# Four accumulator tiles, more idle products, and exponentials read tile by tile from the bank: one change to an attention and gated MLP kernel

## The chip, the cores and the metric

One core of a Trainium2 chip runs the whole program. The metric is the device time of one execution in microseconds (us). TensorE (PE) multiplies, VectorE (DVE), ScalarE (ACT) and GpSimd (POOL) do the elementwise work, and SyncE (SP) issues most transfers. Each engine works through its own list of instructions in order and waits at semaphores for the others.

## The reference

```python
# q, k, v: [8, 8, 576, 64] float32; the head's number sets its mask
scores = q @ k.T / 8
mask_plain = (rel >= 0) & (rel < 32)                                # heads 0 to 3, rel = i - j
mask_dil = (rel >= 0) & (rel < 128) & (rel % 4 == 0)                # heads 4 to 7
scores = where(mask, scores, -1e9); scores -= max(scores)
attn = exp(scores); attn /= sum(attn) + 1e-9
x = (attn @ v) laid out as [4608 tokens, 512]
h = x @ w_in                                                        # w_in [512, 2048]
g = h * sigmoid(1.702 h)
out = g @ w_out                                                     # w_out [2048, 512]
```

The inputs of the MLP arrive as 8-byte floats. They are decoded on the chip into a high and a low part, and every MLP product is the sum of three (high by high, low by high, high by low).

## The kernel before

**Tiling.** Heads are worked on in pairs, four pairs to a batch entry, 32 in all. A pair `k` has scores of 128 rows by 2 heads by 5 tiles (`QT`) of 64 columns. Pairs 0 to 3 (`first_attention`) give the input of the first group of the MLP, so they stand at the head of the program; pairs 4 to 7 (`attention`) are spread over that group, and the other 24 over the later groups. The MLP works in nine groups of 512 tokens: `m0` to `m7` and `r` (the tokens left over). A group runs 16 steps `f`: `up(f)` is 12 products of 512 columns into the bank `hp`, then ACT does a tanh (L605), DVE a gating product (L608), ACT or DVE the high part `gh` and DVE the low part `gl`; `down(f)` adds 12 products into four accumulators of 512 columns each, `acc`. In the last step of a group each accumulator `j` is finished by three products (L633, L634, L637) and drained by ACT into `ost_m` or `ost_r` (L226, from `add_out`), and then stored.

**The accumulators.** All four are one tile, `accs`, of four banks. The first four pairs use the same tile for `first_product` (L462).

**Softmax of pairs 0 to 7** (`masked(k)`): the mask is added by two products with `ident` ahead of the scores, so the bank `sp` holds masked scores. Then DVE takes the maximum (L394), DVE subtracts it (L233, `pr<-sp,mx`, 640 elements), ACT takes the exponential of all 640 (L398), and DVE sums (L412). The bank `sp` is free for the next pair's scores after the subtraction. A reciprocal, a product on POOL or DVE, and DVE transposes into `ct` follow.

**Decoding a weight tile** (`decode`) takes a 512 KB transfer, two ACT shifts (L281, L282), a sign step on DVE or ACT (L277 or L275), and further steps on DVE, ACT and POOL. There are 32 such tiles, all decoded in the head and the first group.

**What sets the order.** `Plan` gathers every operation with a cost for each engine that can do it, and an urgency. `ordered` builds a list for each engine from these costs, once, ahead of the run. So a change of a cost number or an urgency moves instructions between and along the engines. In the head it also puts in `idle` products (L719) on PE where it expects PE to wait: into the bank `hp`, until `up(0)` of the first group has taken that bank.

The names of buffers in the profile are `cell`, `second`, `bt` (undecoded weights), `words` (a decode's middle step), `wih`, `wil`, `woh`, `wol` (decoded weights), `xh`, `xl` (the MLP's input, high and low).

Of the kernel before, what the change touches and what calls it, by code (L numbers as in the profile page):

```python
# [22 lines left out]
AHEAD = 0.6  # L23
WARM = 30.0
# [10 lines left out]
LATER = {PE: 0.0, ACT: 0.0, DVE: 0.4, POOL: 0.0, DMA: 0.0}  # L35
# [3 lines left out]
class Plan:  # L39
# [29 lines left out]
    def ordered(self, warm, warm_until, soon):  # L69
# [24 lines left out]
        while any(open_):  # L94
# [43 lines left out]
def tile_windowed_attention_then_gated_mlp(  # L138
# [49 lines left out]
    accs = bank([P, NC, GT], "acc", "acc")  # L188
# [52 lines left out]
    def decode(n, urgency):  # L241
# [38 lines left out]
        add({DMA: 524}, {0: -7.0, 1: -5.0, 2: -3.5, 3: -2.5}.get(n, urgency), fetch, (), (R, R + "l", *taken))  # L280
# [41 lines left out]
    def load_v(k):  # L322
        u, place = pairs[k], lots(k)[1]

        def work(e):
# [13 lines left out]
            (place, place + "l"), (0.0, 6.0, 8.0, 10.0)[k] if k < NC else 0.0)  # L339
# [38 lines left out]
    def exponentials(k, urgency):  # L378
# [3 lines left out]
        held = ("sp",) if masked(k) else ()  # L382

        def sp():
            return u["all"] if masked(k) else pr

        if not masked(k):
            mine = mask if dilated(k) else plain
            for n, tiles, cost in ((P, slice(0, QT - 1), 0.62), (D, slice(QT - 1, QT), 0.22)):
                add({DVE: cost}, urgency, lambda e, n=n, tiles=tiles: pair(  # L390
                    e, pr[0:n, :, tiles], u["all"][0:n, :, tiles],
                    mine[0:n, None, tiles].broadcast_to([n, 2, tiles.stop - tiles.start, W]), ALU.add),
                    ("sp",), (PR,))
        add({DVE: 0.80}, urgency, lambda e: V.tensor_reduce(out=mx, in_=sp(), axis=AX.X, op=ALU.max),  # L394
            held or (PR,), (MX,))
        add({DVE: 0.80}, urgency, lambda e: pair(
            e, pr, sp(), mx[:, :, :, None].broadcast_to([P, 2, QT, W]), ALU.subtract), (*held, MX), (PR,))
# [8 lines left out]
    def softmax(k, urgency):  # L406
# [5 lines left out]
        add({DVE: 0.80}, urgency, lambda e: V.tensor_reduce(out=sm, in_=pr, axis=AX.X, op=ALU.add), (PR,), (SM,))  # L412
        inverse(k, urgency)
        for a in range(2):
            add({POOL: 0.73, DVE: -0.48}, urgency, lambda e, a=a: pair(
# [30 lines left out]
    def first_product(k):  # L446
# [6 lines left out]
        u["x"] = accs[:, :, ROW * (k % 2):ROW * (k % 2) + ROW]  # L453
# [24 lines left out]
    def drain_x(k, urgency):  # L478
# [19 lines left out]
        if b == 0:  # L498
# [8 lines left out]
            for n, (size, part, src) in enumerate(mains):  # L507
                add({ACT: 0.12 + size * 0.00094}, urgency, lambda e, part=part, src=src: copy(
# [56 lines left out]
    class Group:  # L565
# [119 lines left out]
    for c in range(NC):  # L685
        first_attention(c, c)
        if c in (1, 2):
            decode(c - 1, c + 2.5)
# [79 lines left out]
```

## Time and profile before

| | |
|---|---|
| median of 3 runs | 924.18 us (923.68 to 924.65) |
| the profiled execution | 923.53 us, of which the profile's span is 921.8 us |
| PE busy | 888.0 us (96%) |
| DVE, ACT, POOL busy | 450.3, 386.0, 71.7 us |
| instructions | 17123, of them 7313 products |

PE is busy nearly throughout, so the two places to look at are the stretches in which it is not, and those in which its clock is low. The head of the program (the first 40 us) and the ends of the nine groups are where PE's idle time lies. ACT and DVE are close to full from 40 to 115 us, where the weights are decoded, and half idle later.

### The profile page before, as it was taken

How to read it: one execution, taken by the hardware profiler on the slowest of the kernel's cores; microseconds unless marked ns; L12 is line 12 of the kernel's file. 1: busy time of each engine (PE TensorE's matmuls, PEld its weight loads, DVE VectorE, ACT ScalarE, POOL GpSimd, SP SyncE). 2: the span in 40 equal slices, each digit the busy share in tenths (PEclk: the TensorE clock that was granted, in tenths of full speed). 3: DMA queues.
4: the chain of work that ended last, by engine and by line, in shares of the span. 5: the costliest groups of instructions: out<-in, count | busy, mean ns of one | idle time of the engine just before them, and what ended most of it. 6: DMA issues, size and time to landing. Idle time of an engine off the chain costs nothing.

```text
span 921.8 us, 17123 instructions
## 1 busy us (share of the span) xinstructions
PE 888.0 (96%) x7313; PEld 714.7 (78%) x7313; DVE 450.3 (49%) x844; ACT 386.0 (42%) x669; POOL 71.7 (8%) x86
## 2 busy tenths in 40 slices
PE   6899999999999999999999999999999999999997
PEld 4577777888788878888788878887888778878885
DVE  6799985564556254634564255525422412232221
ACT  5889874343543244323443244424422322232222
POOL 3312220010001000000010000100000000000000
PEclk9799999999999999999999999999999999999999
DMA  9366742211221012300311023101000010001001
GB/s 347 126 223 179 246 134 91 92 46 46 91 92 46 1 64 73 92 0 16 122 46 47 1 91 91 46 1 44 24 1 1 2 44 1 1 14 32 1 1 46
DMA packets 35803, 61.32 MB, mean 67 GB/s; under 512 B 17424, under 2 KB 17680, under 8 KB 35728
## 3 DMA queue, kind: packets, MB, share of 16 engines
q1 hardware_dynamic: 35584, 60.11, 20.3%
q8 instruction: 57, 0.93, 0.4%
q14 instruction: 18, 0.15, 0.1%
q10 hardware_dynamic: 144, 0.13, 0.0%
HBM read 49.48 MB, written 9.44 MB: 64 GB/s over the span
## 4 chain that ended last, share of the span: by engine, by line
PE 90%; ACT 5%; DMA 2%; DVE 1%; issue 1%; SPq 0%; ACTq 0%
PE hp_m L597 37%; PE acc L637 14%; PE acc L633 14%; PE acc L634 13%; PE hp_r L597 5%; PE av L476 3%; PE sp L375 3%; ACT ost_m L226 2%; DMA cell<-wo_dram 1%; PE acc L462 1%; DMA cell<-wi_dram 1%; DMA second<-wo_dram 1%; ACT words L281 1%; ACT second L275 1%; ACT gh L226 0%
## 5 line engine op out<-in xcount | busy, mean ns | idle before, releaser
L633 PE MATMUL acc<-gh,woh 128*128 128x512 f32 x576 | 226.9, 394 | 4.9 <-ACT ost_m L226 4.1
L634 PE MATMUL acc<-gh,wol 128*128 128x512 f32 x576 | 224.4, 390 | 0.0
L597 PE MATMUL hp_m<-xh,wih 128*128 128x512 f32 x512 | 203.8, 398 | 2.8 <-ACT xh L226 1.9
L597 PE MATMUL hp_m<-xl,wih 128*128 128x512 f32 x512 | 201.4, 393 | 0.3 <-DVE xl L233 0.2
L597 PE MATMUL hp_m<-xh,wil 128*128 128x512 f32 x512 | 201.3, 393 | 0.0
L608 DVE SCALAR_TENSOR_TENSOR g_m<-g_m,hp_m 128x512 f32<-128x512 f32 x128 | 87.8, 686 | 230.3 <-ACT g_m L605 229.9
L637 PE MATMUL acc<-gl,woh 128*128 128x512 f32 x576 | 162.3, 394 | 13.7 <-ACT ost_m L226 11.7
L605 ACT ACTIVATE g_m<-hp_m 128x512 f32<-128x512 f32 x128 | 76.6, 599 | 234.4 <-PE hp_m L597 233.9
L637 PEld LDWEIGHTS acc<-gl,woh 128*128 128x128 f32 x576 | 107.6, 188 | 44.3 <-ACT ost_m L226 19.0
L633 PEld LDWEIGHTS acc<-gh,woh 128*128 128x128 f32 x576 | 108.1, 188 | 31.1 <-ACT ost_m L226 6.1
L634 PEld LDWEIGHTS acc<-gh,wol 128*128 128x128 f32 x576 | 108.2, 188 | 21.9
L233 DVE TENSOR_TENSOR gl<-g_m,gh 128x512 fp32r<-128x512 f32 x126 | 89.1, 707 | 58.1 <-ACT gh L226 52.9
L597 PEld LDWEIGHTS hp_m<-xh,wih 128*128 128x128 f32 x512 | 97.0, 190 | 25.5 <-DVE g_m L608 3.1
L597 PEld LDWEIGHTS hp_m<-xl,wih 128*128 128x128 f32 x512 | 97.2, 190 | 22.1 <-DVE xl L233 1.4
L597 PEld LDWEIGHTS hp_m<-xh,wil 128*128 128x128 f32 x512 | 97.1, 190 | 20.1 <-POOL wil L233 0.6
L226 ACT ACTIVATE gh<-g_m 128x512 fp32r<-128x512 f32 x117 | 73.9, 632 | 68.8 <-DVE g_m L608 68.6
L233 POOL TENSOR_TENSOR pr<-pr,sm 128x320 f32<-128x320 f32 x64 | 52.4, 840 | 520.8 <-DVE sm L404 516.6
L226 ACT ACTIVATE bt<-ct 32x320 f32<-32x320 f32 x101 | 47.5, 470 | 14.3 <-DVE ct L425 12.4
L226 ACT ACTIVATE xm<-av 128x512 f32<-128x512 f32 (+2 forms) x42 | 24.5, 594 | 44.8 <-PE av L476 31.5
L608 DVE SCALAR_TENSOR_TENSOR g_r<-g_r,hp_r 128x512 f32<-128x512 f32 x16 | 11.0, 688 | 53.6 <-ACT g_r L605 53.6
L398 ACT ACTIVATE pr<-pr 128x640 f32<-128x640 f32 x32 | 23.7, 740 | 30.9 <-DVE pr L233 30.8
L412 DVE TENSOR_REDUCE sm<-pr 128x10 f32<-128x640 f32 x32 | 26.2, 817 | 13.3 <-ACT pr L398 13.3
(114 smaller groups left out, 717.6 us busy)
## 6 DMA issues: line engine op xcount, KB each, us to landing
qk<-qk_dram SPq DMA_DIRECT2D x17, 576.0 KB, 4.8
out_dram<-ost_m SPq DMA_DIRECT2D x31, 256.0 KB, 2.0
second<-qk_dram SPq DMA_DIRECT2D x13, 576.0 KB, 4.3
v<-vp_dram SPq DMA_DIRECT2D x32, 216.0 KB, 4.3
words<-vp_dram SPq DMA_DIRECT2D x24, 216.0 KB, 4.4
cell<-wi_dram SPq DMA_DIRECT2D x10, 512.0 KB, 5.6
cell<-wo_dram SPq DMA_DIRECT2D x9, 512.0 KB, 4.4
second<-wo_dram SPq DMA_DIRECT2D x6, 512.0 KB, 5.2
```

What stands on the lines that cost most here:

```text
L226: A.activation(dst, src, AF.Copy, scale=scale)
L233: (V if e == DVE else G).tensor_tensor(out=dst, in0=a, in1=b, op=op)
L375: T.matmul(dst[:, w:w + n], u["qk"][rows, at:at + 32], u["qk"][rows, S + first:S + first + n], start=not masked(k), stop=True, tile_positi ...
L398: add({ACT: 0.75}, urgency, lambda e: A.activation(prs[y], prs[y], AF.Exp, scale=0.125), (), (PR,))
L412: add({DVE: 0.80}, urgency, lambda e: V.tensor_reduce(out=sm, in_=pr, axis=AX.X, op=ALU.add), (PR,), (SM,))
L476: T.matmul(dst, u["v"][a][0:KW, m], bt[0:KW, a, m], start=True, stop=True, skip_group_check=True)
L597: T.matmul(hps[f], st[:, f, c], mv[:, c], start=c == 0 and k == 0, stop=c == NC - 1 and k == 2)
L605: A.activation(self.g32, hps[f], AF.Tanh, scale=0.851)
L608: V.scalar_tensor_tensor(out=self.g32, in0=self.g32, scalar=1.0, in1=hps[f], op0=ALU.add, op1=ALU.mult)
L633: T.matmul(self.acc[j], woh[:, f, cols], gh, start=f == 0, stop=False)
L634: T.matmul(self.acc[j], wol[:, f, cols], gh, start=False, stop=False)
L637: T.matmul(self.acc[j], woh[:, f, P * j:P * j + P], self.g[f][1], start=False, stop=f == NF - 1)
```

## The change

1. **Accumulators.** `accs` goes. A tile `first_x` of four banks serves the first four pairs; then its pool is closed, and each accumulator `j` of each group is a tile of its own, in a bank of its own (`quarter`).
2. **Exponentials of pairs 0 to 7.** The subtraction, the one exponential of 640 and the sum go. DVE scales the ten maxima of a row by -0.125 (10 elements), and ACT takes the exponential of each of the 10 tiles straight from the bank `sp`, 64 elements at a time, with the scaled maximum as bias and with the sum as a second output. The bank is free after the last tile.
3. **Idle products.** They go to the bank `av` and may be put in until pair 4's `product` has taken it; the allowance ahead of a wait grows (0.5 us taken off instead of 1.5), and the last planned time from 30 to 36 us.
4. **Numbers of the plan.** Urgencies of the decodes and of pairs 4 to 7, slacks of the first `v`, costs of scores, first products, drains and POOL's product are other numbers. The plan's cost for five tiles of exponentials is 0.80. The up products of the first group wait for both parts of `xh` and `xl`.

```diff
-AHEAD = 0.6
-WARM = 30.0
+AHEAD = 0.70
+WARM = 36.0
...
-                idle = max(0, int((when - max(free[e], 1.2) - 1.5) / (0.28 if when > 5.0 else 0.44)))
+                idle = max(0, int((when - max(free[e], 1.2) - 0.5) / (0.26 if when > 8.0 else 0.44)))
...
-    accs = bank([P, NC, GT], "acc", "acc")
+    four = tc.tile_pool(name="four", bufs=1, space=bass.MemoryType.PSUM)
+    first_x = four.__enter__().tile([P, NC, GT], F32, tag="x", name="first_x")
+
+    def quarter(j, name):
+        if "quarters" not in misc:
+            four.__exit__(None, None, None)
+            misc["quarters"] = ctx.enter_context(tc.tile_pool(name="quarters", bufs=1, space=bass.MemoryType.PSUM))
+        return misc["quarters"].tile([P, GT], F32, tag=f"acc{j}", name=name)
...
-        add({DVE: 0.80}, urgency, lambda e: V.tensor_reduce(out=mx, in_=sp(), axis=AX.X, op=ALU.max),
-            held or (PR,), (MX,))
+        if masked(k):
+
+            sm, SM = sms[y], f"sm{y}"
+            add({DVE: 0.80}, urgency, lambda e: V.tensor_reduce(out=mx, in_=u["all"], axis=AX.X, op=ALU.max),
+                ("sp",), (MX,))
+            add({DVE: -0.15}, urgency, lambda e: V.tensor_scalar(
+                out=mx, in0=mx, scalar1=-0.125, scalar2=None, op0=ALU.mult), (), (MX,))
+            for a in range(2):
+                def tiles_of(e, a=a):
+                    for t in range(QT):
+                        A.activation(pr[:, a, t], u["all"][:, a, t], AF.Exp, bias=mx[:, a, t:t + 1], scale=0.125,
+                                     accum_out=sm[:, a, t:t + 1])
+
+                add({ACT: 0.80}, urgency, tiles_of, ("sp", MX), (PR, SM))
+            return
...
-        add({DVE: 0.80}, urgency, lambda e: V.tensor_reduce(out=sm, in_=pr, axis=AX.X, op=ALU.add), (PR,), (SM,))
+        if not masked(k):
+            add({DVE: 0.80}, urgency, lambda e: V.tensor_reduce(out=sm, in_=pr, axis=AX.X, op=ALU.add), (PR,), (SM,))
...
-                    self.acc[j] = accs[:, j]
+                    self.acc[j] = quarter(j, f"acc_{self.name}_{j}")
...
-                decode(n, 25.0 + 2.3 * n)
+                decode(n, 28.0 + 2.62 * n)
...
-                    attention(NC + c, 50.0 + 10.0 * c)
+                    attention(NC + c, 43.0 + 8.2 * c)
...
-        if 0 not in main[0].hps:
+        if "av" not in pairs[NC]:
             if "idle" not in misc:
-                misc["idle"] = bank([P, GT], "hp", "idle")
+                misc["idle"] = bank([P, GT], "av", "idle")
```

**Where it moves instructions.** First, PE's list at the end of the first group, the last `down` before `up(1)` of the next group, with the semaphores that each row waits for. Before:

```order
L637 MATMUL acc<-gl_75,woh 128x512 [waits Pool_49]
L633 MATMUL acc<-gh_73,woh 128x512
L634 MATMUL acc<-gh_73,wol 128x512
L637 MATMUL acc<-gl_75,woh 128x512 [waits Activation_49]
L633 MATMUL acc<-gh_73,woh 128x512
L634 MATMUL acc<-gh_73,wol 128x512
L637 MATMUL acc<-gl_75,woh 128x512 [waits Activation_49]
L633 MATMUL acc<-gh_73,woh 128x512
```

The same place of the change:

```order
L654 MATMUL acc_m_0_749<-gl_75,woh 128x512 [waits DVE_49]
L650 MATMUL acc_m_1_754<-gh_73,woh 128x512
L651 MATMUL acc_m_1_754<-gh_73,wol 128x512
L654 MATMUL acc_m_1_754<-gl_75,woh 128x512
L650 MATMUL acc_m_2_758<-gh_73,woh 128x512
L651 MATMUL acc_m_2_758<-gh_73,wol 128x512
L654 MATMUL acc_m_2_758<-gl_75,woh 128x512
L650 MATMUL acc_m_3_764<-gh_73,woh 128x512
```

The products stand in the same order; the two waits for ACT among them are gone.

Second, ACT's list in the head, from the first decode step on (buffer numbers 78, 79 are the `pr` of even and odd pairs). Before:

```order
L281 ACTIVATE words<-cell_109 128x512
L282 ACTIVATE cell_109<-cell_109 128x512
L398 ACTIVATE pr_78<-pr_78 128x640
L281 ACTIVATE words<-cell_110 128x512
L398 ACTIVATE pr_79<-pr_79 128x640
L226 ACTIVATE wih<-words 128x512
L282 ACTIVATE cell_110<-cell_110 128x512
L281 ACTIVATE words<-cell_111 128x512
```

The change:

```order
L289 ACTIVATE words<-cell_112 128x512
L290 ACTIVATE cell_112<-cell_112 128x512
L283 ACTIVATE cell_112<-cell_112 128x512
L400 ACTIVATE pr_78,sm_82<-sp_142,mx_80 128x64 x5
L289 ACTIVATE words<-cell_113 128x512
L400 ACTIVATE pr_78,sm_82<-sp_142,mx_80 128x64 x5
L290 ACTIVATE cell_113<-cell_113 128x512
L289 ACTIVATE words<-cell_114 128x512
L290 ACTIVATE cell_114<-cell_114 128x512
L400 ACTIVATE pr_79,sm_83<-sp_230,mx_81 128x64 x5
```

Ten small exponentials stand where one stood, with decode steps among them, and the sign step of the first tile (L283) has come from DVE to ACT. Up to the tanh of the first group's first step, ACT's list has 35 instructions before (from its first decode step on), four of them exponentials; the change has 40 tiles of exponentials and 33 others. On PE, ahead of the first `down`, stand 27 products of `up` before and 33 in the change; and 9 idle products before against 39, of which 15 lie between the scores of pairs 0 and 1, and 10 after the scores of pair 1. On SP the first weight tile's transfer goes from third to second place.

More of the change, by code (lines that the diff above doesn't have):

```diff
@@ L34 @@
 PE, ACT, DVE, POOL, DMA = range(5)
-LATER = {PE: 0.0, ACT: 0.0, DVE: 0.4, POOL: 0.0, DMA: 0.0}
+LATER = {PE: 0.0, ACT: 0.0, DVE: 0.40, POOL: 0.0, DMA: 0.0}
 LATENCY = {PE: 0.3, ACT: 0.2, DVE: 0.2, POOL: 0.2, DMA: 0.2}
@@ L338, in load_v @@
         add({DMA: 390 if k < NC else 442}, (-5.5, -3.0, -2.0, -1.0)[k] if k < NC else 1.6 * k - 0.3, work, waits(k),
-            (place, place + "l"), (0.0, 6.0, 8.0, 10.0)[k] if k < NC else 0.0)
+            (place, place + "l"), (0.0, 1.0, 5.0, 14.0)[k] if k < NC else 0.0)
     def waits(k):
@@ L381, in exponentials @@
         PR, MX = f"pr{y}", f"mx{y}"
[L382 to L394, printed above, removed]
-            held or (PR,), (MX,))
+        if masked(k):
[11 more added lines that the diff above has]
+            return
+        mine = mask if dilated(k) else plain
+        for n, tiles, cost in ((P, slice(0, QT - 1), 0.62), (D, slice(QT - 1, QT), 0.22)):
+            add({DVE: cost}, urgency, lambda e, n=n, tiles=tiles: pair(
+                e, pr[0:n, :, tiles], u["all"][0:n, :, tiles],
+                mine[0:n, None, tiles].broadcast_to([n, 2, tiles.stop - tiles.start, W]), ALU.add),
+                ("sp",), (PR,))
+        add({DVE: 0.80}, urgency, lambda e: V.tensor_reduce(out=mx, in_=pr, axis=AX.X, op=ALU.max), (PR,), (MX,))
         add({DVE: 0.80}, urgency, lambda e: pair(
-            e, pr, sp(), mx[:, :, :, None].broadcast_to([P, 2, QT, W]), ALU.subtract), (*held, MX), (PR,))
+            e, pr, pr, mx[:, :, :, None].broadcast_to([P, 2, QT, W]), ALU.subtract), (MX,), (PR,))
         add({ACT: 0.75}, urgency, lambda e: A.activation(prs[y], prs[y], AF.Exp, scale=0.125), (), (PR,))
@@ L411, in softmax @@
         exponentials(k, urgency)
-        add({DVE: 0.80}, urgency, lambda e: V.tensor_reduce(out=sm, in_=pr, axis=AX.X, op=ALU.add), (PR,), (SM,))
+        if not masked(k):
+            add({DVE: 0.80}, urgency, lambda e: V.tensor_reduce(out=sm, in_=pr, axis=AX.X, op=ALU.add), (PR,), (SM,))
         inverse(k, urgency)
         for a in range(2):
-            add({POOL: 0.73, DVE: -0.48}, urgency, lambda e, a=a: pair(
+            add({POOL: 0.85, DVE: -0.48}, urgency, lambda e, a=a: pair(
                 e, pr[:, a], pr[:, a], sm[:, a, :, None].broadcast_to([P, QT, W]), ALU.mult), (SM,), (f"{PR}.{a}",))
@@ L507, in drain_x @@
             for n, (size, part, src) in enumerate(mains):
-                add({ACT: 0.12 + size * 0.00094}, urgency, lambda e, part=part, src=src: copy(
+                add({ACT: 0.12 + size * (0.0019 if dilated(k) else 0.00094)}, urgency, lambda e, part=part, src=src: copy(
                     e, part(xh[:, c]), src()), FOUR, (f"xh{c}.{n}",))
-                add({DVE: 0.08 + size / 640}, urgency, lambda e, part=part, src=src: pair(
+                add({DVE: 0.08 + size / (490 if dilated(k) else 820)}, urgency, lambda e, part=part, src=src: pair(
                     e, part(xl[:, c]), src(), part(f32(xh[:, c])), ALU.subtract), (*FOUR, f"xh{c}.{n}"), (f"xl{c}.{n}",))
@@ L599, in up @@
             for c in range(NC):
-                split = [f"x{k}{c}.{n}" for k in "hl" for n in range(1)] if self is main[0] else []
+                split = [f"x{k}{c}.{n}" for k in "hl" for n in range(2)] if self is main[0] else []
                 add({PE: 0.681}, 0.0, lambda e, c=c: product(c), (f"wi{f}", f"xh{c}", f"xl{c}", *split), (place,))
@@ L687, in tile_windowed_attention_then_gated_mlp @@
         if c in (1, 2):
-            decode(c - 1, c + 2.5)
+            decode(c - 1, c + 0.1)
     last, nxt = None, 1
```

10 lines of the change are left out of this document (5 added, 5 removed).

## The prediction

> **What bounds the kernel now.** I read the page's first lines, then the waits of TensorE (PE), then the timeline around the longest group of waits, then busy time by stretches.
>
> ```profile
> span 921.8 us, 17123 instructions
> PE 888.0 (96%) x7313; PEld 714.7 (78%) x7313; DVE 450.3 (49%) x844; ACT 386.0 (42%) x669; POOL 71.7 (8%) x86
> ```
>
> PE is the bound over the whole run, so a gain has to come from its 34 us of idle time or from stretches in which it runs slowly. The view of waits names the idle time (total, times, longest):
>
> ```profile
> PE acc L637 <- ACT ost_m L226: 11.7, 17, 0.7
> PE acc L633 <- ACT ost_m L226: 4.1, 6, 0.7
> PE acc L637 <- ACT ost_r L226: 2.1, 3, 0.7
> PE acc L462 <- issue: 2.0, 1, 2.0
> PE hp_m L597 <- ACT xh L226: 1.9, 2, 1.2
> PE hp_m L597 <- DVE g_m L608: 0.7, 1, 0.7
> PE acc L633 <- ACT gh L226: 0.6, 2, 0.3
> ```
>
> The first three lines are 26 waits of 0.69 us: products into the accumulators that wait for ACT to drain one. They all lie at ends of groups. The timeline of the last one (start, length, instruction, idle time before it) shows what one costs:
>
> ```profile
> 138.86 0.60 ACT L226 ACTIVATE ost_m<-acc 128x512 f32<-128x512 f32 x1 [0.47 <-PE acc L634]
> ...
> 915.37 0.50 PE L637 MATMUL acc<-gl,woh 128*128 128x512 f32 x1 [0.69 <-ACT ost_m L226]
> 915.71 0.39 PE L633 MATMUL acc<-gh,woh 128*128 128x512 f32 x1
> 915.94 0.40 PE L634 MATMUL acc<-gh,wol 128*128 128x512 f32 x1
> 917.03 0.50 PE L637 MATMUL acc<-gl,woh 128*128 128x512 f32 x1 [0.69 <-ACT ost_m L226]
> ```
>
> A product follows the one before it after 0.23 us (915.71 to 915.94). Where the wait is, the step is 1.09 us (915.94 to 917.03), and the step after a wait is 0.34 us (915.37 to 915.71). So one wait costs 0.86 + 0.11 = 0.97 us, more than the 0.69 us that is called idle, since the pipeline runs empty. The product that waits goes into another accumulator than the one being drained: the drain starts when the next accumulator's first products end (the 0.47 us wait for L634 at 138.86), and the third product of that accumulator waits for the drain. That is an order among accesses to one tile, not one that the data need.
>
> Busy time by stretches, cut at ACT's first decode step, at the first, eighth and sixteenth tanh of the first group (columns: length, PE, PEld, DVE, ACT, POOL busy and instructions, clock, DMA share, GB/s):
>
> ```profile
> 8.13:38.93 30.80, 24.81 (x641) 16.84 (x642) 23.43 (x49) 22.34 (x35) 12.05 (x12) 0.83 0.63 238
> 38.93:77.11 38.18, 37.27 (x305) 29.21 (x304) 35.47 (x67) 35.47 (x55) 6.64 (x6) 1.00 0.57 181
> 77.11:132.75 55.64, 54.87 (x571) 42.78 (x570) 50.15 (x97) 46.59 (x77) 9.96 (x10) 1.00 0.73 219
> 132.75:921.80 789.05, 766.92 (x5706) 624.04 (x5704) 337.98 (x623) 279.08 (x500) 41.76 (x51) 1.00 0.13 41
> ```
>
> In the head PE is idle for a fifth of the time and waits for the softmax of pairs 0 to 3. In the second row PE is nearly full, but ACT and DVE are at 93% too: what is added there to one of them turns soon into time. In the third row ACT has 9 us to spare, in the last one more than half.
>
> **The accumulators.** With a tile for each, the 26 waits go: 26 x 0.97 = 25.2 us. What is late next? A drain takes 0.60 us and the three products of an accumulator 3 x 0.23 = 0.69 us, so ACT keeps pace behind PE. The next group's first product into the same bank now waits for that drain, but 12 products of `up(1)` (2.7 us) stand between. The next group's `gh` needs tanh, gating product and copy behind up to four drains on ACT, some 4 us after `up(0)`; PE has 24 products (5.5 us) in between. I take no new wait.
>
> **The exponentials: DVE.** For each of eight pairs the subtraction and the sum go, and a product of ten elements comes:
>
> ```profile
> 7.40 0.82 DVE L233 TENSOR_TENSOR pr<-sp,mx 128x640 f32<-128x640 f32 x1
> ...
> 10.04 0.82 DVE L412 TENSOR_REDUCE sm<-pr 128x10 f32<-128x640 f32 x1
> 10.77 0.81 DVE L394 TENSOR_REDUCE mx<-sp 128x10 f32<-128x640 f32 x1
> 11.50 0.16 DVE L402 TENSOR_SCALAR sm<-sm 128x10 f32<-128x10 f32 x1
> ```
>
> From start to start a large one takes 0.73 us, so DVE is relieved of 2 x 0.73 - 0.16 = 1.3 us a pair. This shortens nothing by itself, since ACT gets the work.
>
> **The exponentials: ACT.** The one exponential of 640 goes and ten of 64 come. Nothing in the trace shows an exponential with a bias read from memory or with a sum. The nearest rows are a copy of 64 elements out of a bank, and the exponential:
>
> ```profile
> 20.99 0.23 ACT L226 ACTIVATE xr<-acc 128x64 f32<-128x64 f32 x1
> 21.09 0.64 ACT L226 ACTIVATE woh<-words 128x512 fp32r<-128x512 f32 x1
> 21.62 0.70 ACT L281 ACTIVATE words<-bt 128x512 f32<-128x512 f32 x1
> ...
> 12.70 0.73 ACT L398 ACTIVATE pr<-pr 128x640 f32<-128x640 f32 x1
> 13.32 0.62 ACT L226 ACTIVATE wih<-words 128x512 fp32r<-128x512 f32 x1
> ...
> 15.42 1.33 ACT L275 ACTIVATE cell<-cell 128x512 f16<-128x512 f32 x1
> 16.50 0.72 ACT L282 ACTIVATE cell<-cell 128x512 uint32<-128x512 uint32 x1
> ```
>
> The copy holds ACT for 0.10 us until the next starts, and lasts 0.23 us by itself. So a tile, T, costs at least 0.10 us; and if each runs alone, and giving out its sum takes a further instruction of that size, 0.46 us. I take the middle, 0.28 us, since both additions cost something and nothing says that they prevent all overlap. A pair is then 2.8 us on ACT in place of 0.62 us.
>
> The Trainium skill, "ScalarE: Activation LUTs", section "What ACT_TABLE_LOAD costs", says that a bias read through a pointer adds about 93 ns to an ACTIVATE and that neighbours overlap by about 93 ns; by its figures a tile would be an estimated 0.24 us, and the time predicted below 2.4 us less (60 tiles x 0.04); it has no price for the sum that is given out.
>
> *In the head.* ACT's list from its first decode step to the first tanh was 35 instructions, 22.3 us, of which the four exponentials were 4 x 0.62. The change has 33 others: two more of some 0.55 us and a little, so about 21.4 us, and 40 tiles. It can start earlier, since the first weight tile is fetched second:
>
> ```profile
> 8.13 0.67 ACT L281 ACTIVATE words<-cell 128x512 f32<-128x512 f32 x1 [2.91 <-DMA cell<-wi_dram]
> ...
> 38.93 0.60 ACT L605 ACTIVATE g_m<-hp_m 128x512 f32<-128x512 f32 x1 [0.88 <-PE hp_m L597]
> ...
> 41.73 0.50 PE L633 MATMUL acc<-gh,woh 128*128 128x512 f32 x1
> ...
> 5.00:10.00 5.00, 4.15 (x172) 2.70 (x177) 2.67 (x4) 2.09 (x4) 0.00 (x0) 1.00 1.02 408
> ```
>
> The 0.59 MB that now come after it are 1.4 us at 408 GB/s, so ACT starts at 6.7. With 1.2 us of waiting (it had single waits above 2 us before; I take about half of one) the first tanh comes at 6.7 + 21.4 + 40 x 0.28 + 1.2 = 40.5 us, against 38.93: 1.6 us later. Following the softmax of the four pairs by hand gives the same: each pair holds the bank longer, but after the fourth ACT still has some 8 us of decode steps and copies ahead of the tanh. The first `down` follows 2.8 us after the tanh, as now. By then PE has done 33 instead of 27 products of `up`: 6 x 0.23 = 1.4 us that needn't be done later. Head: +0.2 us.
>
> *Up to the eighth tanh.* ACT's list loses a sign step (1.08 us, 15.42 to 16.50), two exponentials and a copy (0.53, 21.09 to 21.62; together about 2.8 us) and gains 20 tiles (5.6 us). ACT goes from 35.5 to 38.3 us. PE would need 38.2 - 1.4 = 36.8 us there. So ACT, full, takes the head's gain back: +1.5 us. Up to the sixteenth, the list loses seven instructions besides the exponentials, and the 20 tiles fill that; the 9 us of room cover it. If that room were gone, it would be up to 3 us.
>
> **The idle products.** They were 0.43 us apart (an inference from two taking 1.03 us and three 1.46 us), so the 15 between the scores of pairs 0 and 1 fill 6.5 us, from 6.5 to 13.0:
>
> ```profile
> 6.44 1.03 PE L719 MATMUL idle<-ident 128*128 128x512 bf16 x2
> ...
> 27.00:28.00 1.00, 0.99 (x3) 0.56 (x3) 1.00 (x3) 1.00 (x2) 0.00 (x0) 0.51 0.81 319
> 36.00:37.00 1.00, 1.00 (x4) 0.71 (x4) 1.00 (x2) 1.00 (x3) 0.00 (x0) 0.50 0.00 0
> 37.00:38.00 1.00, 1.00 (x5) 0.87 (x4) 1.00 (x3) 1.00 (x2) 0.00 (x0) 0.88 0.00 0
> ```
>
> The second scores wait for the first ten tiles of exponentials, until about 12.6, so the products are hidden; with tiles of 0.10 us they would hold the scores up by 2 us. What they may buy is the clock, which was granted at half from 27 to 37 us. I count that as nothing: after the change ACT's list, not PE, decides when the tanh comes.
>
> The Trainium skill, "TensorE: Matmul & The Clock Gate", Part 1, has the clock fall to half after an idle window of about 3.4 us and return after as long a busy one. The trace has the fall at 27 us after waits of 2.0 us at most, so it does not need one unbroken pause here; by that rule the change would keep PE at full clock, and the rival of short tiles below is where it would count.
>
> **The rest.** The products on POOL that go to DVE (25, at the plan's choice) fall in the last stretch, where DVE is busy 338 of 789 us. SP fetches the same bytes; pair 3's scores now come at about 25 us, later than any of the moved transfers at this rate. The wait for both parts of `xh` was kept by order already.
>
> **Sum.** 921.8 - 25.2 + 0.2 + 1.5 = 898.3 us of span. Around the span lie 1.7 us (the profiled execution took 923.53), and that execution is 0.65 us below the median of 924.18. So the median would be 898.3 + 2.4 = 900.7; I say 900.5 us.
>
> **The rivals.**
> - *Short tiles.* T near 0.15, so ACT is not the bound of the head: tanh at 6.7 + 21.4 + 6 + 1.2 = 35.3, 3.6 us sooner, the six products' 1.4 us kept, and the clock helping to keep up: 921.8 - 25.2 - 5.0 = 891.6, 894 us. At T = 0.10 it would be 892. For it speaks the 0.10 us row; against it, that it leaves 0.05 us for bias and sum together.
> - *Long tiles.* T = 0.46: tanh at 47.7, +8.8 - 1.4; the second stretch's ACT 32.7 + 9.2 = 41.9 against 36.8, +5.1 at most; so 921.8 - 25.2 + 12 = 909, 911 us. For it: ACT's small instructions stand alone at 0.23 us.
> - *The waits stay.* If drains and products were held apart by the bank memory rather than by the tile, 924 + 1.7 = 926 us or, with half of the waits gone, 913. Against it: the drained accumulator and the written one are different banks before, too, and `hp` is read by ACT while PE writes `acc` without a wait.
> - *Slower.* ACT's tiles cost so much that the head and the second stretch eat the 25.2 us: 40 + 20 tiles, 60 x (T - 0.28) = 23.5, T = 0.67 us, three times the 0.23 us of a lone copy. From there on it is slower than before: at 0.75 us, 900.7 + 60 x 0.47 = 929 us. Nothing in the rows comes near it.
>
> **How the numbers follow.** My forecast (T from 0.2 to 0.36: 896 to 906) has 0.60, short tiles 0.20, long ones 0.14, waits that stay wholly or by half 0.04, slower through ACT 0.02. About 0.2% (1.9 us) is what a measurement here can tell from no change; only the last two cases come near that line: faster 0.95, same 0.02, slower 0.03. The range 892 to 908 leaves out the ends of short and long tiles and the last two cases, together about 0.2.
>
> **What would show it.** No wait of a product for `ost_m` or `ost_r`, and 12 products at a group's end in 2.7 us, would show the first step right. The ten tiles of a pair on ACT give T: 2.8 us if I am right, under 2 or above 4 us if a rival is. The first tanh at about 40.5 us and ACT above 95% up to the eighth would show the second step. The clock before 37 us shows what the idle products do. I am wrong if the head moves by more than 4 us either way, or if ends of groups show another wait in place of the drains.

## The result and the profile after

The changed kernel takes 902.3 us (median of four runs, 901.18 to 903.96) against 924.25 us for the kernel before beside it: ratio 0.9764, 95% interval 0.9747 to 0.9781. The forecast was 900.5 us, in a range from 892 to 908. The profiled execution of the change took 903.96 us, the slowest of its four, 1.7 us above the median; the times of events below are from it.

The page's first lines, then the view of waits of PE (total, times, longest):

```profile
span 902.2 us, 17350 instructions
...
PE 884.7 (98%) x7343; PEld 718.5 (80%) x7343; DVE 457.3 (51%) x859; ACT 397.8 (44%) x824; POOL 50.0 (6%) x60
```

```profile
PE sp L369 <- ACT pr L400: 3.5, 3, 1.8
PE hp_m L614 <- DVE g_m L625: 2.3, 3, 1.1
PE sp L383 <- issue: 2.2, 1, 2.2
PE hp_m L614 <- ACT xh L234: 2.0, 1, 2.0
```

The lines with `ost_m` and `ost_r` are gone. What heads the list now are scores that wait for exponentials on ACT (`sp` for `pr`); before, scores waited for DVE instead, twice 0.8 us. The timeline of PE at the end of the last group, the place of the prediction's second fence:

```profile
896.65 0.39 PE L651 MATMUL acc_m<-gh,wol 128*128 128x512 f32 x1
896.88 0.39 PE L654 MATMUL acc_m<-gl,woh 128*128 128x512 f32 x1
897.10 0.39 PE L650 MATMUL acc_m<-gh,woh 128*128 128x512 f32 x1
897.33 0.39 PE L651 MATMUL acc_m<-gh,wol 128*128 128x512 f32 x1
```

The products follow each other after 0.23 us, across accumulators too. Now the head, from the timeline of ACT and PE (start, length, idle time before):

```profile
6.54 0.67 ACT L289 ACTIVATE words<-cell 128x512 f32<-128x512 f32 x1 [1.33 <-DMA cell<-wi_dram]
...
6.71 5.37 PE L736 MATMUL idle<-ident 128*128 128x512 bf16 x15
...
12.52 0.43 PE L369 MATMUL sp<-plain,ident 128*128 128x320 bf16 x2 [0.44 <-ACT pr L400]
...
14.58 0.68 ACT L289 ACTIVATE words<-cell 128x512 f32<-128x512 f32 x1 [1.56 <-DMA cell<-wi_dram]
...
19.36 0.43 PE L369 MATMUL sp<-early,ident 128*128 128x320 bf16 x2 [1.83 <-ACT pr L400]
...
22.62 0.92 PE L383 MATMUL sp<-xm 64*32 64x64 f32 x41 [2.19 <-issue]
...
25.68 0.32 ACT L400 ACTIVATE pr<-sp,mx 128x64 f32<-128x64 f32 x1 [2.50 <-DVE mx L395]
...
28.80 0.69 PE L369 MATMUL sp<-early,ident 128*128 128x320 bf16 x2 [1.22 <-ACT pr L400]
...
44.85 0.58 ACT L622 ACTIVATE g_m<-hp_m 128x512 f32<-128x512 f32 x1
...
50.26 0.63 PE L650 MATMUL acc_m<-gh,woh 128*128 128x512 f32 x1
```

The first tanh stands at 44.85 us (38.93 before), the first `down` at 50.26 (41.73 before). Busy time by stretches (columns as in the prediction), cut at ACT's first decode step and at the first, eighth and sixteenth tanh:

```profile
6.54:44.85 38.31, 29.63 (x688) 17.63 (x675) 26.10 (x60) 32.93 (x113) 8.67 (x9) 0.82 0.58 213
44.85:88.37 43.52, 42.27 (x418) 32.79 (x417) 38.66 (x73) 39.20 (x93) 5.05 (x5) 0.92 0.69 206
88.37:140.15 51.78, 50.73 (x455) 40.82 (x454) 44.47 (x84) 46.72 (x109) 6.41 (x6) 1.00 0.69 197
```

The account is simplest when it is cut at the last `down` of the first group. That starts at 145.39 us, against 137.53 before: 7.9 us lost. From there to the last product are 752.2 us, against 779.5 (917.03 - 137.53): 27.3 us won. The tail is 0.1 us shorter. Together 19.5 us, and the spans differ by 921.8 - 902.2 = 19.6.

### The profile page after: what moved, and what is told of

Its sections match the earlier page's. It is cut to its first block, busy times and chain, and to the rows that moved or that the text cites. A ratio compares the mean times of both kernels' runs of the same rounds, so it can differ in the third digit from the quotient of the medians.

```text
span 902.2 us, 17350 instructions
## 1 busy us (share of the span) xinstructions
PE 884.7 (98%) x7343; PEld 718.5 (80%) x7343; DVE 457.3 (51%) x859; ACT 397.8 (44%) x824; POOL 50.0 (6%) x60
## 4 chain that ended last, share of the span: by engine, by line
PE 91%; ACT 3%; DVE 3%; DMA 1%; issue 1%; SPq 0%; ACTq 0%
PE hp_m L614 37%; PE acc_m L650 12%; PE acc_m L654 12%; PE acc_m L651 12%; PE hp_r L614 5%; PE av L493 3%; PE sp L383 3%; ACT pr L400 2%; PE acc_r L654 2%; PE acc_r L651 2%; PE acc_r L650 2%; DMA cell<-wi_dram 1%; DVE words L295 1%; DVE wol L241 0%; DVE words L293 0%
## 5 line engine op out<-in xcount | busy, mean ns | idle before, releaser
L650 PE MATMUL acc_m<-gh,woh 128*128 128x512 f32 x512 | 201.5, 394 | 0.0
L651 PE MATMUL acc_m<-gh,wol 128*128 128x512 f32 x512 | 199.7, 390 | 0.0
L654 PE MATMUL acc_m<-gl,woh 128*128 128x512 f32 x512 | 143.0, 391 | 0.0
L614 PEld LDWEIGHTS hp_m<-xl,wih 128*128 128x128 f32 x512 | 96.8, 189 | 22.3 <-DVE xl L241 1.9
L650 PEld LDWEIGHTS acc_m<-gh,woh 128*128 128x128 f32 x512 | 96.4, 188 | 20.8
L651 PEld LDWEIGHTS acc_m<-gh,wol 128*128 128x128 f32 x512 | 96.4, 188 | 19.7
L654 PEld LDWEIGHTS acc_m<-gl,woh 128*128 128x128 f32 x512 | 95.7, 188 | 20.3
L234 ACT ACTIVATE gh<-g_m 128x512 fp32r<-128x512 f32 x110 | 69.6, 633 | 67.1 <-DVE g_m L625 66.8
L241 POOL TENSOR_TENSOR pr<-pr,sm 128x320 f32<-128x320 f32 x45 | 40.4, 909 | 549.4 <-DVE sm L420 516.8
L414 ACT ACTIVATE pr<-pr 128x640 f32<-128x640 f32 x24 | 17.7, 739 | 38.8 <-DVE pr L241 38.8
L622 ACT ACTIVATE g_r<-hp_r 128x512 f32<-128x512 f32 x16 | 9.6, 598 | 50.8 <-PE hp_r L614 50.8
```

The costliest lines, as they stand in the source:

```text
L234: A.activation(dst, src, AF.Copy, scale=scale)
L241: (V if e == DVE else G).tensor_tensor(out=dst, in0=a, in1=b, op=op)
L414: add({ACT: 0.75}, urgency, lambda e: A.activation(prs[y], prs[y], AF.Exp, scale=0.125), (), (PR,))
L614: T.matmul(hps[f], st[:, f, c], mv[:, c], start=c == 0 and k == 0, stop=c == NC - 1 and k == 2)
L622: A.activation(self.g32, hps[f], AF.Tanh, scale=0.851)
L650: T.matmul(self.acc[j], woh[:, f, cols], gh, start=f == 0, stop=False)
```

## The experiments

Each is timed in five rounds against the kernel before on the same chip. All at a glance; "ACT" is its busy and idle time from its first decode step to the first tanh, "rest" the time from the last `down` of the first group to the last product, in the profiled execution:

| kernel | ratio (95%) | first tanh | ACT | last `down` of first group | rest |
|---|---|---|---|---|---|
| before | 1 | 38.93 | 22.3, 8.5 | 137.53 | 779.5 |
| the change | 0.9764 (0.9747 to 0.9781) | 44.85 | 32.9, 5.4 | 145.39 | 752.2 |
| four accumulators alone | 0.9704 (0.9689 to 0.9720) | 40.03 | 22.1, 10.0 | 139.11 | 752.5 |
| all but the accumulators | 1.0048 (1.0034 to 1.0063) | 44.55 | 33.0, 5.4 | 143.75 | 778.7 |
| change, old exponentials | 0.9733 (0.9718 to 0.9747) | 41.10 | 27.6, 6.9 | 143.23 | 752.2 |
| change, old idle products | 0.9759 (0.9744 to 0.9774) | 45.19 | 33.3, 5.8 | 144.69 | 752.2 |
| change, cost of tiles 1.45 | 0.9757 (0.9743 to 0.9772) | 43.33 | 34.6, 2.1 | 142.84 | 752.5 |
| change, idle products in pieces | 0.9753 (0.9738 to 0.9768) | 44.32 | 32.9, 5.0 | 142.36 | 752.5 |
| change, sums on DVE | 0.9792 (0.9774 to 0.9809) | 43.95 | 34.0, 3.6 | 144.93 | 752.1 |
| accumulators and tiles | 0.9760 (0.9745 to 0.9774) | 43.64 | 32.7, 3.5 | 141.70 | 752.7 |
| accumulators, tiles for pairs 4 to 7 | 0.9726 (0.9705 to 0.9748) | 39.83 | 22.2, 10.2 | 141.05 | 752.8 |
| accumulators, tiles for pairs 0 to 3 | 0.9763 (0.9742 to 0.9783) | 44.20 | 32.6, 3.6 | 141.69 | 752.4 |
| accumulators, new idle products | 0.9701 (0.9680 to 0.9721) | 38.29 | 22.0, 8.5 | 138.85 | 752.4 |
| accumulators, tiles for pairs 0 to 3, two more banks for pair 1 | 0.9725 (0.9712 to 0.9739) | 40.47 | 29.1, 3.6 | 139.90 | 752.8 |

The last column falls into two classes, one for each way of holding the accumulators. Everything else of the change acts in the first 145 us. One thing to keep in mind for all of them: the plan makes its lists anew for each kernel, so an edit also moves decode steps ahead of the first tanh or behind it. The column of ACT shows by how much.

**Four accumulators alone.** The kernel before with this and nothing more:

```diff
-    accs = bank([P, NC, GT], "acc", "acc")
...
+    first_x = four.__enter__().tile([P, NC, GT], F32, tag="x", name="first_x")
...
+    def quarter(j, name):
...
-                    self.acc[j] = accs[:, j]
+                    self.acc[j] = quarter(j, f"acc_{self.name}_{j}")
```

> The kernel before with the four accumulator tiles alone; plan, softmax and idle products as before. Theory of the waits (26 waits at 0.97 us are the whole gain, and the rest of the change costs some 3 us in the head): 924.2 - 25.2 = 899 us, head as before (first tanh at 38.9, first down at 41.7 us), no wait for a drain. Rival (the waits are worth only the 22 us that the whole change gained, and the rest is neutral): 902.3 us.

Measured: 897.79 us, ratio 0.9704, better than the change as a whole. In the timeline the first group's end, from the first of its 12 products to the next product of `up`, now lasts 2.72 us, where it was 4.67 with two waits:

```profile
139.11 0.39 PE L640 MATMUL acc_m<-gh,woh 128*128 128x512 f32 x1
...
141.83 0.39 PE L604 MATMUL hp_m<-xh,wih 128*128 128x512 f32 x1
```

So two waits cost 1.95 us, 0.98 each. The whole rest shrinks by 27.0 us.

**All but the accumulators.** The change with one tile for the four accumulators, as before:

```diff
-                    self.acc[j] = quarter(j, f"acc_{self.name}_{j}")
+                    self.acc[j] = accs[:, j]
```

> The change with one accumulator tile as before; exponentials by tiles, idle products and the plan's numbers stay. Theory of the waits: the waits are back, 902.3 + 25.2 = 927.5 us, slower than before by about 3 us, which is the price of the rest. Rival (rest neutral): 924 us.

Measured: 929.64 us, ratio 1.0048: 0.5% slower than before, with 1 outside the interval. The waits are back, 26 of them:

```profile
PE acc L646 <- ACT ost_m L226: 11.0, 16, 0.7
...
PE acc L642 <- ACT ost_m L226: 4.8, 7, 0.7
...
PE acc L646 <- ACT ost_r L226: 2.1, 3, 0.7
```

The two runs show that the whole gain, and more, is the accumulators', and that the other three parts together cost about 4.4 us (0.0048 x 925; 3.1 to 5.8 by the interval), or 5.5 by the distance of the change from the accumulators alone (0.0060).

**The change with the old exponentials.** Subtraction, one exponential and sum for pairs 0 to 7, all else as in the change:

```diff
-        if masked(k):
...
-                add({ACT: 0.80}, urgency, tiles_of, ("sp", MX), (PR, SM))
-            return
         add({DVE: 0.80}, urgency, lambda e: pair(
...
+            e, pr, sp(), mx[:, :, :, None].broadcast_to([P, 2, QT, W]), ALU.subtract), (*held, MX), (PR,))
```

> The change with the softmax of pairs 0 to 7 as before (subtraction, one exponential of 640, sum); accumulators, idle products and the plan's other numbers stay. Theory that ACT's list sets the head (40 tiles x 0.29 us in place of 4 x 0.62): the list up to the first tanh is 9 us shorter, so the tanh comes at about 39 to 41 instead of 44.9 us and the time is 898 to 899 us. Rival (DVE's 1.3 us a pair pay for ACT's load): 903 us or slower. Second rival (the plan's other numbers cost the head its 3 us): 902 us, no change.

Measured: 900.77 us, ratio 0.9733. The tanh is back at 41.10 us, and the time 2.9 us below that of the change (0.0031 x 924); the intervals just meet. ACT had 27.6 us of work ahead of it instead of 32.9: 9.1 us less of exponentials, and 3.8 us more of decode steps that the plan put there. It is still 2.7 us above the accumulators alone: the new numbers of the plan have a price of their own when the exponentials are the old ones.

**The change with the old idle products.** They are also back in the bank `hp`, until the first `up` has taken it:

```diff
-WARM = 36.0
+WARM = 30.0
-                idle = max(0, int((when - max(free[e], 1.2) - 0.5) / (0.26 if when > 8.0 else 0.44)))
+                idle = max(0, int((when - max(free[e], 1.2) - 1.5) / (0.28 if when > 5.0 else 0.44)))
```

> The change with the idle products placed as before (bank hp, until the first up, allowance of 1.5 us, last planned time 30 us); the rest stays. Theory that ACT's list sets the head: within 1.5 us of 902.3, with the clock at half for longer. Rival (the clock counts): PE at half speed up to the first down costs 2 to 4 us, 904 to 906 us. Second rival (idle products hold up the scores): 1 to 2 us faster.

Measured: 903.09 us, ratio 0.9759, no difference from the change, although the granted clock was at half for longer, from 20.5 to 40.9 us.

**The true cost in the plan.** Five tiles take 1.45 us on the chip (below); the plan has 0.80.

```diff
-                add({ACT: 0.80}, urgency, tiles_of, ("sp", MX), (PR, SM))
+                add({ACT: 1.45}, urgency, tiles_of, ("sp", MX), (PR, SM))
```

> The change with one number altered: the plan counts five tiles of exponentials as 1.45 us (5 x 0.29, as measured) in place of 0.80. Theory that the plan's wrong price costs time (it expects the bank sp back 1.3 us too early for each pair and puts work in the wrong order): 1 to 3 us faster than the change's 902.3, ratio 0.973 to 0.975. Rival (ACT's load itself counts, whatever the order): within 1 us, ratio 0.976.

Measured: 901.78 us, ratio 0.9757: not told apart from the change. This execution happened to keep the clock up to the tanh. From 18 to 42 us, here and then in the change:

```profile
18.00:42.00 24.00, 17.34 (x472) 10.88 (x472) 18.23 (x43) 22.36 (x74) 7.56 (x7) 1.00 0.38 133
```

```profile
18.00:42.00 24.00, 17.57 (x459) 11.21 (x458) 15.49 (x40) 20.22 (x71) 5.09 (x6) 0.72 0.35 119
```

With a granted clock of 1.00 instead of 0.72 the tanh still comes at 43.33 us, so the clock is not the main cause of the late tanh. The plan, which now knows what the tiles cost, leaves ACT only 2.1 us idle, but fills the time with other work (34.6 us busy), and the tanh gains 1.5 us.

**Idle products in pieces.** 24 of the idle products are issued as three each (columns in the proportion 2, 1, 1), so that the product at which PE stops in pair 2's scores is another one:

```diff
-            T.matmul(misc["idle"], ident, ident[:, None, :].broadcast_to([P, GT // P, P]), start=True, stop=True)
+            misc["n"] = misc.get("n", 0) + 1
+            for at, n in ((0, 2), (2, 1), (3, 1)) if 5 < misc["n"] <= 29 else ((0, 4),):
+                T.matmul(misc["idle"][:, P * at:P * at + P * n], ident, ident[:, None, :].broadcast_to([P, n, P]),
+                         start=True, stop=True)
```

> The change with 24 of the idle products cut in three pieces of the same total columns, so that 48 more products stand ahead of pair 2's scores. In all traces so far PE stops some 2 us at its 351st or 352nd product, whatever that product is. Theory (PE's instructions come late there, and in the change this stop lies on the path of pair 2): the stop now falls where PE waits for ACT anyway, and the time falls by 1.5 to 2.2 us, to 900.1 to 900.8, ratio 0.974; the trace shows the stop, if at all, at the products with ident ahead of pair 2's scores. Rival (ACT's list hides it): 902.3, ratio 0.976. Second rival (the stop belongs to the product, not to its number): it stays in the scores of pair 2.

Measured: 901.08 us, ratio 0.9753. The stop of 2.19 us is gone; two short ones, 0.83 and 0.44 us, stand elsewhere:

```profile
24.70 1.16 PE L479 MATMUL first_x<-ct,second 32*64 32x64 f32 x59 [0.44 <-issue]
...
29.52 0.51 PE L383 MATMUL sp<-xr 64*32 64x64 f32 x21 [0.83 <-issue]
```

The gain of about 1 us lies within the intervals: not resolved.

**Sums on DVE.** The tiles stay on ACT, without the second output; DVE sums 640 elements as before.

```diff
-                                     accum_out=sm[:, a, t:t + 1])
...
-        if not masked(k):
+        if True:
             add({DVE: 0.80}, urgency, lambda e: V.tensor_reduce(out=sm, in_=pr, axis=AX.X, op=ALU.add), (PR,), (SM,))
```

> The change with the sums of pairs 0 to 7 back on DVE (one reduction of 640 elements a pair), exponentials still by tiles with their bias. A tile on ACT should then take 0.20 us instead of 0.29. Theory that ACT's list sets the head: 40 x 0.09 = 3.6 us less on ACT ahead of the first tanh, 0.8 us more on DVE's path for each pair: 1 to 3 us faster, ratio 0.973 to 0.975. Rival (the softmax's chain of waits sets the head, and DVE is on it): no change or slower, ratio 0.976 or more.

Measured: 904.09 us, ratio 0.9792, if anything slower than the change. The timeline of ACT gives the price of a tile without a sum:

```profile
8.75 1.08 ACT L400 ACTIVATE pr<-sp,mx 128x64 f32<-128x64 f32 x5
9.69 0.70 ACT L289 ACTIVATE words<-cell 128x512 f32<-128x512 f32 x1
```

Five tiles take 9.69 - 8.75 = 0.94 us, 0.19 each. With a sum, in the change, each tile is two instructions:

```profile
9.14 0.31 ACT L400 ACTIVATE pr<-sp,mx 128x64 f32<-128x64 f32 x1
9.34 0.20 ACT L400 ACTIVATION_READ_ACCUMULATOR pr<-sp,mx 128x1 f32 x1
9.43 0.32 ACT L400 ACTIVATE pr<-sp,mx 128x64 f32<-128x64 f32 x1
```

From tile to tile 0.29 us, of which the separate reading of the sum is 0.10. So 40 tiles without it save ACT about 4 us ahead of the tanh, and the tanh comes only 0.9 us sooner. That does not tell the two theories apart, since the plan gave ACT as much other work as the sums had taken: it was busy for 33.97 us up to the tanh (32.93 in the change), and for 118.3 up to the sixteenth (118.9):

```profile
6.39:43.95 37.56, 30.97 (x699) 18.10 (x685) 28.66 (x62) 33.97 (x76) 7.81 (x7) 0.86 0.59 223
6.39:139.69 133.30, 124.74 (x1569) 91.56 (x1555) 113.05 (x221) 118.34 (x239) 24.28 (x23) 0.94 0.64 205
```

What less work on ACT would bring has not been measured.

**Accumulators and tiles, old numbers and idle products.** The kernel of the first experiment, with the change's exponentials for pairs 0 to 7:

```diff
+                add({ACT: 0.80}, urgency, tiles_of, ("sp", MX), (PR, SM))
+            return
```

> The kernel before with the accumulator tiles and the exponentials by tiles; idle products and the plan's numbers as before. Theory that the tiles' load on ACT costs about 3 us whatever the plan's numbers (as between e3_old_exp and the change): ratio 0.9704 + 0.003 = 0.9735. Rival (the new numbers go with the tiles, and without them the tiles cost more): ratio 0.978 or more. Second rival (under the old numbers the tiles pay): 0.969 or less.

Measured: 901.69 us, ratio 0.9760, equal to the change. So under the old numbers the tiles cost 0.9760 - 0.9704 = 0.0056, 5.2 us, and under the new ones 2.9 us. The new numbers and idle products give nothing when there are tiles, and cost something when there are none. What lies in the numbers was not tried number by number.

**Tiles for pairs 4 to 7, and for pairs 0 to 3.** The same kernel, with the tiles for one half of the pairs; the other half goes the old way. A condition `tiled(k)` stands where `masked(k)` did for the branch of the tiles:

```diff
+    def tiled(k):
+
+        return NC <= k < FIRST * NC
...
+        if tiled(k):
```

> The kernel before with four accumulator tiles, and exponentials by tiles for pairs 4 to 7 alone. With tiles for all eight pairs the same kernel was at 901.7 us (0.976 of before), with tiles for none at 897.8 (0.970), so tiles cost 5.2 us. Theory, the head: the bank of scores is held until the last tile, each of pairs 1 to 3 starts later, and the first tanh comes 3.6 us later; pairs 4 to 7 cost nothing or up to 1 us. Then this is 897.5 to 899 us, ratio 0.970 to 0.972, first tanh at 40. Rival, ACT's list: twenty tiles at 0.29 us less four exponentials of 0.6 us are 3.3 us more on a full ACT between the first tanh and the eighth, and they are the cost: 900.5 to 901.5 us, ratio 0.973 to 0.975.

```diff
+    def tiled(k):
+
+        return k < NC
...
+        if tiled(k):
```

> The kernel before with four accumulator tiles, and exponentials by tiles for pairs 0 to 3 alone. Theory, the head: nearly all of the tiles' 5.2 us is here, so 901 to 903 us, ratio 0.974 to 0.976, first tanh at 43 to 45 us, scores of pair 3 at 27 to 29 us instead of 20. Rival, ACT's list after the first tanh: this is 898 to 899.5 us, ratio 0.970 to 0.972, since work that PE does ahead in the head makes up for a late tanh.

Measured: 899.40 us, ratio 0.9726, and 902.65 us, ratio 0.9763. Tiles for the first four pairs alone cost as much as tiles for all eight. For pairs 4 to 7 the ratio is not told apart from none; the trace shows 2.1 us from the first tanh to the last `down` of the group (141.05 - 39.83 = 101.2, against 139.11 - 40.03 = 99.1).

**New idle products with the accumulators.** The first experiment's kernel with the change's three edits on idle products (allowance, bank, last planned time):

> The kernel before with four accumulator tiles and the change's idle products (other allowance, bank av, planned time to 36 us); no tiles, old numbers of the plan. The changed kernel without tiles was 2.7 us slower (0.9733) than four accumulators alone (0.9704); what of its numbers or idle products costs that is open. Theory: idle products move nothing by themselves, as they did in the changed kernel: 897 to 899 us, ratio 0.970 to 0.972, and the 2.7 us are the urgencies'. Rival: longer idle products push the scores or the first up products back: 900 to 901 us, ratio 0.973 to 0.974. Other rival: they hold the granted clock at full through the head and save 1 to 3 us: 895 to 897 us.

Measured: 897.03 us, ratio 0.9701: no difference from the accumulators alone, and so not what costs 2.7 us in the kernel with old exponentials. It is the lowest time of all, equal with the first experiment's within the intervals.

**Two more banks for pair 1.** Tiles for pairs 0 to 3, but pair 1's scores stand in `av` and `hp`, free at that time, so that they don't wait for pair 0's last tile, nor pair 2's for pair 1's:

```diff
+    def apart(k):
+
+        return k == 1
...
+        if apart(k):
+            u["box"] = [bank([P, GT], n, f"sp_{n}_{k}")[:, 0:QT * W].rearrange("p (t w) -> p t w", t=QT)
+                        for n in ("av", "hp")]
```

> The kernel before with four accumulator tiles and exponentials by tiles for pairs 0 to 3 (902.7 us, 0.9763), but pair 1's scores go into two other banks, av and hp, one for each head, so that they needn't wait for pair 0's last tile, nor pair 2's for pair 1's; the maximum of pair 1 is two reductions, and idle products end ahead of its scores. ACT has the same 40 tiles ahead of the first tanh. Theory, the held bank: with one bank the products waited 2.8, 2.1 and 1.2 us for the tiles; two of the three waits go, scores of pairs 1 and 2 start 3 us earlier or more, the first tanh comes at 40 to 42.5 us instead of 44.2, and the time is 898.5 to 900.5 us, ratio 0.972 to 0.974. Rival, the work on ACT: 40 tiles take 11.6 us wherever they stand, and the first tanh waits for ACT's list: tanh at 43.5 to 45 us, 901.5 to 903.5 us, ratio 0.975 to 0.978.

Measured: 899.16 us, ratio 0.9725 (0.9712 to 0.9739), against 0.9763 (0.9742 to 0.9783) with one bank. Scores of pairs 1, 2 and 3 and the first tanh, with one bank:

```profile
12.20 0.43 PE L372 MATMUL sp<-plain,ident 128*128 128x320 bf16 x2 [2.81 <-ACT pr L403]
...
19.30 0.69 PE L372 MATMUL sp<-early,ident 128*128 128x320 bf16 x2 [2.06 <-ACT pr L403]
...
27.67 0.69 PE L372 MATMUL sp<-early,ident 128*128 128x320 bf16 x2 [1.18 <-ACT pr L403]
...
44.20 0.60 ACT L632 ACTIVATE g_m<-hp_m 128x512 f32<-128x512 f32 x1
```

And with two more banks:

```profile
6.26 0.45 PE L380 MATMUL sp_av<-plain,ident 128*128 128x320 bf16 x1
...
12.05 0.69 PE L380 MATMUL sp<-early,ident 128*128 128x320 bf16 x2 [3.67 <-ACT pr L416]
...
21.78 0.69 PE L380 MATMUL sp<-early,ident 128*128 128x320 bf16 x2 [2.54 <-ACT pr L416]
...
40.47 0.60 ACT L646 ACTIVATE g_m<-hp_m 128x512 f32<-128x512 f32 x1 [1.50 <-PE hp_m L638]
```

The same 40 tiles stand ahead of the tanh in both. The scores come 6 to 7 us sooner, the tanh 3.7 us, the median time 3.5 us (0.0038 x 924). But the plan also moved five of ACT's other steps behind the tanh. Up to the first tanh and up to the sixteenth, with one bank and then with two more:

```profile
7.98:44.20 36.22, 23.23 (x649) 16.33 (x648) 22.52 (x52) 32.61 (x112) 10.14 (x11) 0.76 0.56 211
7.98:136.55 128.57, 113.22 (x1520) 88.17 (x1519) 108.34 (x204) 113.86 (x247) 25.24 (x25) 0.93 0.62 201
```

```profile
7.83:40.47 32.64, 19.89 (x586) 15.20 (x569) 19.91 (x48) 29.08 (x108) 9.73 (x11) 0.90 0.62 228
7.83:134.66 126.83, 111.13 (x1457) 86.89 (x1440) 107.61 (x204) 114.85 (x248) 31.74 (x30) 0.97 0.64 209
```

Up to the first tanh ACT is idle for 3.6 us in both, and has 3.5 us less to do with two more banks: the tanh comes sooner by what this list is shorter. Up to the sixteenth, ACT has as much to do in both (247 and 248 instructions) and is idle for 12.0 us instead of 14.7, and this tanh comes 1.9 us sooner: so the opened bank does give back waiting time. How much of the 3.5 us is the bank's and how much the order's is not separated. The clock was also better kept (0.90 against 0.76 up to the first tanh), but at a like mean clock over the run, 0.986, the times were 902.35 and 903.23 us with one bank and 899.98 with two more. PE still shows waits for tiles, since it now stands ready sooner; a wait in that list is not by itself a loss. This kernel also has fewer idle products, which the other two runs on them show to be worth nothing. It is still about 2 us above the accumulators alone, with intervals that overlap.

## Why the prediction was right, and where it was off

**Right for the reason given: the boundaries.** No wait for a drain is left, and 12 products take 2.72 us. Four middle groups, from the last `down` of the second to that of the sixth, took 639.14 - 241.09 = 398.0 us before and 632.86 - 246.73 = 386.1 after: 11.9 us for 12 waits, 0.99 each, where 0.97 was read from one timeline. The rest as a whole gave 27.3 us against 25.2. Of that, 26 x 0.99 = 25.8 us are the waits, and about 1.6 us the clock: before, it was granted at half once in the rest, right behind three drain waits, and nine products took 3.64 us there (644.74 to 648.38) instead of 9 x 0.23 = 2.1:

```profile
644.82:648.24 3.42, 3.42 (x10) 2.68 (x9) 0.00 (x0) 0.60 (x1) 0.00 (x0) 0.50 0.41 153
```

In the change PE is busy for all of the rest (752.17 of 752.17 us), at a granted clock of 1.00. That nothing new waits at the ends was right. The Trainium skill, "PSUM — Partial Sum Buffer", section "PSUM bank collisions raise a hardware error", has the rule to guard this memory by bank and quadrant; the kernel before guarded four banks as one, and the runs give the price of that here: about 1 us a wait.

**Right: the tile on ACT.** 0.29 us measured, 0.28 taken. The middle was composed of a bias and a sum of unknown price; they are 0.09 (0.19 less the copy's 0.10) and 0.10 us. The Trainium skill's 93 ns for a bias through a pointer ("ScalarE: Activation LUTs", "What ACT_TABLE_LOAD costs") agrees with the 0.09. The estimate of 0.24 us by its figures lies 0.05 above the 0.19 measured without a sum and 0.05 below the 0.29 with one, of which 0.10 is the separate instruction that reads the sum. The rivals of short and long tiles fell with this number.

**Off: the head.** By the prediction's own sign it was wrong here: the first tanh moved by 5.9 us, and more than 4 was to mean a mistake. The step that failed is the waiting term of the first tanh, 1.2 us. ACT began at 6.54 us (6.7 forecast) and was busy for 32.93 us up to the tanh (21.4 + 40 x 0.28 = 32.6 forecast); but the stretch lasted 38.31 us, so it was idle for 5.4 us. The forecast took ACT's list as the bound: of the 8.5 us for which ACT had been idle before, the tiles were to fill all but 1.2, and they filled 3.1. Of the 5.4 us, 1.56 are a wait for a late weight tile and 2.50 the wait for the maximum of pair 2. That maximum was late because the scores of pair 2 waited 1.83 us for the tiles of pair 1 and PE then stopped for 2.19. So the scores of pair 3 came at 28.80 us, where the forecast had about 25. The sentence that following the four pairs by hand gives the same was the wrong one.

The chain is: ACT's tiles of pair k end, the bank comes free, PE writes scores of pair k + 1, DVE takes the maximum, ACT goes on. One bank makes a ring of it, and a stop of PE or a late weight tile anywhere in it is passed on. The view of the chain that ends at the first `down` runs through this ring from 15.7 to 30.9 us, and from 36.8 to 46.2 through DVE's list, decode steps above all; some of its rows (start, length, what, how many):

```profile
17.83 1.49 ACT pr L400 x10
...
20.43 2.19 issue
...
25.68 2.13 ACT pr L400 x14
...
39.48 0.57 DVE words L295
```

That the ring costs something is shown by the run with two more banks, which gave ACT 2.7 us of waiting back up to the sixteenth tanh. That the ring alone makes the tanh late is not shown: the run with sums on DVE left ACT as much work as before, the two banks came with another order, and the part of the chain on DVE was not tested.

**Off: after the tanh.** 2.8 us to the first `down` were forecast, as before; in the profiled execution it was 5.4 us, as the clock was at half there:

```profile
45.00:51.00 6.00, 5.26 (x13) 3.78 (x12) 5.90 (x12) 6.00 (x10) 0.00 (x0) 0.50 0.98 308
```

This row is of the change's slowest execution; with idle products in pieces the same stretch had a granted clock near 1.00, and 3.6 us from tanh to `down` (44.32 to 47.89). From the first tanh to the last `down` of the group the change took 100.5 us against 98.6: +1.9, where the terms for that stretch (1.4 us of products done ahead, 1.5 us of ACT's list) gave +0.1. With idle products in pieces it was 98.0 us (142.36 - 44.32), so the +1.9 is more likely that execution's clock than the change. The term for twenty tiles itself, +1.5, is near the 2.1 us of the run with tiles for pairs 4 to 7 alone. The sign named for it, ACT above 95% up to the eighth tanh, did not come: it was busy for 39.2 of 43.5 us, 90%.

**Right: the idle products.** Fifteen filled 6.71 to 12.08 us (5.4 us, where 6.5 was forecast), and the scores behind them still waited 0.44 us for tiles; the new ones are not told apart from the old ones, in two pairs of runs. The Trainium skill's rule on the clock ("TensorE: Matmul & The Clock Gate", Part 1, an idle window of about 3.4 us) would have had them hold it. In the change the granted clock was at half from about 21 to 35 us, with no wait longer than 2.2 us there: measured, it falls without so long an unbroken pause (in the kernel before, at 644.82 us, behind pauses of 0.69 us). As forecast, the clock is worth little while PE waits for softmax; right behind the first tanh, at half, it cost the profiled execution nearly 2 us.

**The sum.** Head and first group: +7.9 us instead of +1.7 in this execution, which was itself 1.7 us above its median; rest: -27.3 instead of -25.2. The two errors are of opposite sign, so it is in part luck that the median lies only 1.8 us above the forecast.

## What to carry to other kernels

Look at what a semaphore guards: where one tile covers several banks, draining one holds up the writing of another, and a tile for each bank gave back 1 us per drain here at no cost. Before work is moved from one engine to another in a stretch full of waits, forecast the waits too, pair by pair: who holds the buffer between the engines, and until when. The sum of busy times on the fullest engine gave its busy time within 0.4 us, and missed its idle time by 4. Try the parts of a change alone: the first part by itself was faster than the whole. And where a program orders the instructions, look in each trial's trace at what it moved: two trials here were meant to differ in one thing and differed in the order as well.

## What was unexpected of the hardware

In nearly every trace of this kernel, PE stops in the head for no reason that the profile shows ("issue"), at its 351st or 352nd product, whatever that is: 2.0 us before, 2.19 in the change, 1.97 to 2.42 in the kernels with all but the accumulators, old exponentials, old idle products and sums on DVE, 1.25 to 1.89 in the kernels built from the one before, 0.30 with the true cost of tiles. Smaller stops follow some 127 products later (1.1 us with old exponentials), which with the weight loads is 254 to 256 instructions. The page's table of DMA queues fits that:

```profile
q8 instruction: 57, 0.93, 0.4%
```

57 packets of 0.93 MB / 57 = 16.3 KB, and PE has 2 x 7343 = 14686 instructions, 258 to a packet. The traces have the time of each packet: in all 20 stops of the fourteen traces up to 60 us, PE goes on 1.2 to 1.6 us after the end of a packet of this queue (in the change it ran from 20.15 to 21.26, and PE went on at 22.62; before, from 17.30 to 18.42, and PE went on at 19.79). This is strong evidence that PE waits there for its own instructions, which arrive in such packets. Why a packet comes late is inferred and not shown: weights are being fetched just then (DMA share 1.02 from 5 to 20 us). With idle products in pieces, where other work stands at the 352nd product, no stop was left there, and the two short ones stood at the 479th and the 607th.

A granted clock that falls in the head does so at other times in each execution (half from 21 to 35 us in the change, from 19 to 39 with accumulators alone, not at all from 18 to 42 with the true cost of tiles), and times of one kernel spread by 1 to 4 us. Differences below about 2 us between these kernels are therefore not told from nothing here.
